# Two-layer decode attention: where the last batch's second-layer values are loaded, and when batches 0 to 6 are finished

## The chip, the core and the metric

The kernel runs on one core of a Trainium2 chip. The metric is the device time of one execution in microseconds (us). Six runs of the kernel before took 1181.73 to 1190.4 us, with a median of 1183.62 us. One execution was also profiled; all instruction times below are from it and count from its first instruction.

The core has engines that run side by side, each through its own instructions in order: PE (matmuls; PEld is its weight loads), DVE (vector), ACT (scalar), POOL (GpSimd) and SP, which here only issues DMAs. They wait for one another by semaphores.

## What is computed

Eight sequences ("batches") of one new token each pass through two layers. Both layers have the same weights and read the same key and value caches:

```
x = A_x                                    # 8 x 1 x 512
for layer in (1, 2):
    x = x + attention(layernorm(x))        # wq, K cache, V cache, wo
    x = x + silu(layernorm(x) @ w1) @ w2   # w1: 512 x 1792, w2: 1792 x 512

attention: q = (x @ wq) in 32 heads of 128; 8 groups of K and V, 4 heads each
           p = softmax(q . K * 128**-0.5)  over 8192 cached positions
           o = p . V ; result = o @ wo     # wo: 4096 x 512
```

Everything is bfloat16. For one batch and one group, K and V are 8192 x 128, that is 2 MB each. Layer 2 of a batch needs the batch's own layer 1, so values are read twice from HBM. Keys are read once, because a batch's eight groups stay on the chip between the layers.

## The kernel before

**Storage.** `kts` holds eight key slots of 2 MB, one per group. `ring` holds seven cells of 0.5 MB, of which the plan hands out six; values, four wq pieces per batch (the half of wq for groups 4 to 7) and layer-1 wo pieces go through it, in loads of one cell or of two neighbouring cells. The other half of wq, w1 and w2 stay on the chip. There are seven buffers for probabilities, `ps`: three used in turn (`N_P`) and four for deferred units (`N_DEF`).

**One unit of work** is (layer, batch, group), in two steps. `keys` (L698) expands the query (L721), spreads it into block form (L729, DVE), computes scores from the key slot (L746, 32 matmuls in four parts), takes the maximum (L758 to L767, with an all-reduce on POOL), the exponential (L772, ACT), and brings the probabilities into their buffer (L778 on PE, L785 on DVE). `values` (L819) loads V in four quarters and multiplies (L842, 8 matmuls per quarter), then reduces to one vector per head (L852, L856, L864) and normalises (L874 in layer 2). In layer 1 `turns` (L687) first transposes a key slot in place (L694).

**Passes.** The loop variable `b` runs from -1 to 7. A pass mixes layer 2 of batch `b` with layer 1 of batch `b`+1. In the middle passes the values of four second-layer groups, 4 to 7, are put off ("held") to the start of the next pass. There they load while the batch's chain runs: output of layer 1 (L960, L963), FFN (`ffn_nodes`, L481), the next norm (`norm_nodes`, L410), and the queries `queries_0` (groups 0 to 3, L642) and `queries_1` (groups 4 to 7, L665, with the four wq pieces). The pass of `b` = 7 has no layer 1 of another batch. Its order of loads is: the 16 single cells held from batch 6, single cells for groups 0 and 1 of batch 7, four wq pieces, pairs of cells for the other groups, with all of wo (two loads of 2 MB into key slots 0 and 2, `load_wo_all`, L968) put in before the sixth group.

**The end.** All eight batches' second-layer heads lie in `qab`. Eight out projections (`out_proj_b`, L924, matmuls at L933), one per group and for eight batches at once, add up in one PSUM tile. Then come the residual add (L1049), one norm and FFN for eight batches, a turn (L1058), a copy (L1066) and the store (L1080).

**The order** is not written out by hand. Each step is a node with an engine, a planned duration, a priority and dependencies. `Plan.run` (L172) plays the nodes through: each engine takes the ready node of the lowest priority number, loads go strictly in the order in which they were added, a ring load also needs free cells and gets their numbers, and a load is planned to have landed `LAND` after its transfer. The planned duration of a PE node is multiplied by `PE_SLOW`. The order that comes out is emitted once, and is then fixed for each engine. On the chip semaphores alone decide when an instruction starts. SP waits before each load until its cells or its slot were last read.

```
n = Node(name, eng, dur * (self.PE_SLOW if eng == "PE" else 1), emit, prio, deps)          # L150
heapq.heappush(events, (wire + self.LAND, seq, "done", n))                                 # L209
order = plan.run(range(N_CELL - 1))                                                        # L1071
```

Of the kernel before, what the change touches and what calls it, by code (L numbers as in the profile page):

```python
# [14 lines left out]
N_P = 3  # L15
N_DEF = 4
# [119 lines left out]
class Plan:  # L136
# [1 line left out]


    RATE = {1: 2.57, 2: 2.51, 4: 2.48}  # L140
    LAND = 2.0
    HOP = 0.1
    PE_SLOW = 1.15

    def __init__(self):
        self.nodes = []
# [104 lines left out]
def _build(ctx, nc, A_x, A_k_cache, A_v_cache, A_wq, A_wo, B_w1, B_w2, out):  # L251
# [65 lines left out]
    syn = Sync(nc, ctx)  # L317
    ksem = [DmaCounter(syn.new_sem(f"kt{i}")) for i in range(G)]
    rsem = [DmaCounter(syn.new_sem(f"ring{i}")) for i in range(N_CELL)]
    wsem = {n: DmaCounter(syn.new_sem(f"w_{n}")) for n in ("w1", "w2", "x", "wq0")}  # L320
    osem = syn.new_sem("osem")

    table = {}
# [33 lines left out]
    def gran(i, cells=1):  # L357
        return ring[:, i * GR:(i + cells) * GR]
# [51 lines left out]
    def norm_nodes(tag, prio, b0, nb, deps):  # L410
# [49 lines left out]
        def apply():  # L460
            if nb == 1:
                op(dve, lambda: dve.tensor_scalar(
                    xn[:, b0, :], xs[:, b0, :], nm, rstd[:, 0:1], op0=ALU.add, op1=ALU.mult),
                    reads=[res("xs"), res("misc"), res("rstd")], writes=[res("xn")])
            else:
                nmb = nm.unsqueeze(2).to_broadcast([128, nb, KT])
                rs = rstd[:, 0:nb].unsqueeze(2).to_broadcast([128, nb, KT])
                op(dve, lambda: dve.tensor_tensor(big_x, xs[:, bs, :], nmb, ALU.add),
                   reads=[res("xs"), res("misc")], writes=[res("ring", 1)])
                op(dve, lambda: dve.tensor_tensor(xn[:, bs, :], big_x, rs, ALU.mult),  # L470
                   reads=[res("ring", 1), res("rstd")], writes=[res("xn")])

        a = plan.add(f"{tag}.stats", "PE", 0.3, stats, prio, deps)
# [7 lines left out]
    def ffn_nodes(tag, prio, b0, nb, deps):  # L481
        bs = slice(b0, b0 + nb)
        hp = MI[:, 0:FT * nb]
        yp = MI[:, 256:256 + KT * nb]
        th, hs = (th1[:, :], hs1[:, :]) if nb == 1 else (big_th, big_hs)
        own = [] if nb == 1 else [res("ring", 1)]

        def up():
            steps = []
            for ft in range(FT):  # L490
                for kt in range(KT):
                    steps.append(lambda ft=ft, kt=kt: pe.matmul(
                        hp[:, ft * nb:(ft + 1) * nb], w1_sb[:, kt, ft * 128:(ft + 1) * 128], xn[:, bs, kt],
                        start=(kt == 0), stop=(kt == KT - 1)))
            mms(steps, reads=[res("w1"), res("xn")], writes=[res("misc")])

        def tanh():
            op(act, lambda: act.activation(th, hp, ACT.Tanh, scale=0.5),
               reads=[res("misc")], writes=[res("th")] + own)

        def gate():
            op(dve, lambda: dve.scalar_tensor_tensor(
                hs, th, 1.0, hp, op0=ALU.add, op1=ALU.mult),
                reads=[res("misc"), res("th")], writes=[res("hs")])

        def down():
            steps = []
            for dt in range(KT):
                for ft in range(FT):
                    steps.append(lambda dt=dt, ft=ft: pe.matmul(  # L510
                        yp[:, dt * nb:(dt + 1) * nb], w2_sb[:, ft, dt * 128:(dt + 1) * 128],
                        hs[:, ft * nb:(ft + 1) * nb], start=(ft == 0), stop=(ft == FT - 1)))
            mms(steps, reads=[res("w2"), res("hs")], writes=[res("misc")])

        def resid():
            yv = yp.rearrange("p (k b) -> p b k", b=nb)
            op(dve, lambda: dve.scalar_tensor_tensor(
                xs[:, bs, :], yv, 0.5, xs[:, bs, :], op0=ALU.mult, op1=ALU.add),
                reads=[res("misc"), res("xs")], writes=[res("xs")])

        n = norm_nodes(tag + ".ln", prio, b0, nb, deps)
        u = plan.add(f"{tag}.up", "PE", 1.65, up, prio, [n] + ffn_deps)
        t = plan.add(f"{tag}.tanh", "ACT", 0.2, tanh, prio, [u])
        g = plan.add(f"{tag}.gate", "DVE", 0.18, gate, prio, [t])
        d = plan.add(f"{tag}.down", "PE", 1.65, down, prio, [g])
        return plan.add(f"{tag}.resid", "DVE", 0.18, resid, prio, [d])
# [168 lines left out]
            tn.append(plan.add(f"t{b}.{g}.{q}", "DVE", T_TURN, turn, count[0] + 0.5, [kn] + tn[-1:]))  # L695
        kept[b, g] = tn

    def keys(layer, b, g, q_dep, late=None, first=False):  # L698

        u = count[0]  # L700
        count[0] += 1
        pr = FIRST + 4 if first else u
        tn = kept[b, g]
        if late is None:
            sm = plain[0] % N_P
            plain[0] += 1
        else:
            sm = N_P + late
# [29 lines left out]
        for q in range(4):  # L738
            def score(q=q):
# [3 lines left out]
                for y in range(2):  # L743
                    for t in range(4):
# [2 lines left out]
                            sc[32 * t:32 * t + 32, 0:256], w, kv[:, 2 * t + y, q],  # L747
                            start=(q == 0 and y == 0), stop=(q == 3 and y == 1)))
                mms(steps, reads=[res("kt", g), res("bd", u % N_BD)], writes=[res(*scr)], add=(q > 0))
            sn.append(plan.add(f"s{u}.{q}", "PE", 0.3, score, pr - 1,  # L750
                               [tn[3], bn] + sn[-1:]))

        if layer == 1:
# [62 lines left out]
    ot_users = []  # L816
    es = []

    def values(h, wo=None, cells=2):  # L819

        layer, b, g, u, sm = h["layer"], h["b"], h["g"], h["u"], h["sm"]
        pr = count[0] - 1
        pt, o = ps[sm], len(ot_users) % N_OT
        ot = OT[o]
        hd = slice(R * g, R * g + R)
# [2 lines left out]
        for P in range(4):  # L828
            if P == (2 if cells == 2 else 3) and wo is not None:
                h["wo"] = load_wo(wo)  # L830
            if P % cells == 0:
                vn = load_v(b, g, P, cells)

            def pv(P=P, vn=vn):


                vt = gran(vn.give, cells).rearrange("p (a c t n) -> p a c t n", a=cells, c=2, t=4)[:, P % cells]
                steps = []
                for c in range(2):
                    for t in range(4):  # L840
# [1 line left out]
                        steps.append(lambda t=t, c=c, k=k: pe.matmul(  # L842
                            ot[32 * t:32 * t + 2 * R, 0:2 * DH], pt[:, k:k + 2 * R], vt[:, c, t],
                            start=(P == 0 and c == 0), stop=(P == 3 and c == 1)))
                mms(steps, reads=cells_of(vn) + [res("p", sm)], writes=[res("ot", o)], add=(P > 0))
            n = plan.add(f"v{u}.{P}", "PE", 0.35, pv, pr, [h["exp"], vn, old or clear_n] + vs[-1:])
            if P % cells == cells - 1:
                frees(n, vn)
            vs.append(n)

# [70 lines left out]
        frees(n, wn)  # L921
        return n

    def out_proj_b(h, wn, prev):  # L924

        g = h["g"]

        def mul():
            w = slot(2 * (g // 4)).rearrange("p (h d) -> p h d", h=16)
            steps = []  # L930
            for r in range(R):
                for dt in range(KT):
                    steps.append(lambda r=r, dt=dt: pe.matmul(  # L933
                        YT[:, dt * NB:(dt + 1) * NB], w[:, R * (g % 4) + r, dt * 128:(dt + 1) * 128],
                        qab[:, :, R * g + r],
                        start=(g == 0 and r == 0 and dt == 0), stop=(g == G - 1 and r == R - 1),
                        skip_group_check=True))
            mms(steps, reads=[res("wo_all", g // 4)] + [res("attnb", g, b) for b in range(NB)],
                writes=[res("yt")], add=g > 0)
        return plan.add(f"e.w{g}", "PE", 0.56, mul, count[0] - 3, [h["n"], wn, prev])  # L940


    free_yt = [None]
# [14 lines left out]
    def x2_node(b, prio):  # L958
# [5 lines left out]
               reads=[res("ysum"), res("xs")], writes=[res("xs")])  # L964
        return plan.add(f"c{b}.x2", "DVE", 0.3, add, prio, [y_now[0]])

    wo_all = []
    def load_wo_all():  # L968
        for i in range(2):
            n = plan.load(f"woall{i}", 4, None, scored[2 * i], ring=False)  # L970

            def emit(i=i):
                dma(sp, slot(2 * i).rearrange("p (h d) -> p h d", h=16), wo_v[:, 16 * i:16 * i + 16, :], ksem[2 * i],
                    writes=[res("kt", 2 * i), res("wo_all", i)])

            n.emit = emit
            wo_all.append(n)
# [19 lines left out]
    for b in range(-1, NB):  # L997
        ready = None
        prio = FIRST
        if b >= 0:  # L1000
# [5 lines left out]
            for h in held:  # L1006
                values(h, cells=1)
                ends.append(h)
        ks, vs, held_units = pass_of(b)
        made = {}  # L1010
        todo = list(ks)

        def advance(unit):
            while unit not in made:
                k = todo.pop(0)
                layer, kb, g = k
                if layer == 0:
# [2 lines left out]
                        load_wq0()  # L1020
                        first_q.update(queries_0("f", FIRST, 0, NB, [f5]))
                    if kb == 0 and g == 4:
                        first_q.update(queries_1("f", count[0] - 5, 0, NB, [f5]))
                    made[k] = keys(0, kb, g, first_q[g])
                else:
                    if g == 4:
                        second_q.update(queries_1(f"c{b}", count[0] - 3, b, 1, [ready]))
                    made[k] = keys(1, kb, g, second_q[g], held_units.index(k) if k in held_units else None, g == 0)

        for i, v in enumerate(vs):  # L1030
            advance(vs[min(i + (1 if i == 0 and b >= 0 else 2), len(vs) - 1)])
            if b == NB - 1 and i == 5:
                load_wo_all()
            if v[0] == 0:
                a_values(made[v], cells=1 if b >= 0 and i >= len(vs) - 3 else 2)
            else:
# [4 lines left out]
            load_ffn()  # L1041


    w = free_yt[0]
    for h in ends[-G:]:
        w = out_proj_b(h, wo_all[h["g"] // 4], w)

    def e_x2():
        op(dve, lambda: dve.tensor_tensor(  # L1049
            xs[:, :, :], YT[:, 0:KT * NB].rearrange("p (k b) -> p b k", b=NB), xs[:, :, :], ALU.add),  # L1050
            reads=[res("yt"), res("xs")], writes=[res("xs")])

    big = count[0] + 10
    n = plan.add("e.x2", "DVE", 0.2, e_x2, big, [w])
    n = ffn_nodes("e", big, 0, NB, [n])

    def e_turn():
        steps = [lambda kt=kt: pe.matmul(  # L1058
# [51 lines left out]
```

## Time and profile before

| What | Value |
|---|---|
| Median of six runs | 1183.62 us |
| The profiled execution | 1184.53 us |
| Its span, first to last instruction | 1182.8 us |
| PE busy | 706.7 us (60%) |
| DVE busy | 597.7 us (51%) |
| ACT busy, POOL busy | 136.9 us, 116.8 us |
| HBM read | 465.05 MB |
| Issue to landing, median: V one cell, V two cells, a key slot | 8.2, 11.1, 11.3 us |

A row of the profile's groups reads "line engine op out<-in, shape, count, busy time, mean of one, idle time before it and who ended that". The chain of waits follows the work that ended last back to the start. In the timeline a line has the start, the duration, the engine, the line of the code and, in brackets, how long the engine had been idle and whose event ended that. "x17" after an SP line means 17 issues merged, with the waits between them in the duration.

### The profile page before, as it was taken

What the parts mean: (1) busy time and instruction counts of PE and PEld (TensorE: products, weight loads), DVE (VectorE), ACT (ScalarE), POOL (GpSimd) and SP (SyncE); (2) the same over time, 40 slices, a digit from 0 to 9 for tenths busy, and PEclk for the clock granted to TensorE, in tenths of its full rate; (3) what the DMA queues carried; (4) which work ended last, traced back from release to release, by engine and by line L of the source; (5) the groups of instructions that cost most, each with busy time, mean ns of one, the idle gap of its engine ahead of it and who ended that gap; (6) DMA issues with size and microseconds to landing.
All of it is one profiled execution on the core that took longest, in us unless ns stands there. A gap on an engine that the chain in (4) does not pass through costs nothing.

```text
span 1182.8 us, 31675 instructions
## 1 busy us (share of the span) xinstructions
PE 706.7 (60%) x13588; PEld 369.7 (31%) x13588; DVE 597.7 (51%) x1713; ACT 136.9 (12%) x475; POOL 116.8 (10%) x295
## 2 busy tenths in 40 slices
PE   2544555675565755666565766568556575666754
PEld 1222332242332423323232333224233242332433
DVE  5652467625564355733657245752556436563321
ACT  0010011111111110111111111111111111111110
POOL 1000011100110000100111000110001001010110
PEclk9666677656685666856667567775768666675775
DMA  9999799999999999999999999999999999999994
GB/s 365 421 420 353 314 421 424 411 398 409 419 416 384 382 356 415 424 406 395 420 421 411 397 408 421 421 404 405 413 402 417 390 405 422 411 405 410 347 356 177
DMA packets 86413, 467.13 MB, mean 395 GB/s; under 512 B 8944, under 2 KB 14848, under 8 KB 61952
## 3 DMA queue, kind: packets, MB, share of 16 engines
q1 hardware_dynamic: 86272, 465.10, 97.7%
q8 instruction: 107, 1.75, 0.6%
q14 instruction: 34, 0.28, 0.1%
HBM read 465.05 MB, written 0.01 MB: 393 GB/s over the span
## 4 chain that ended last, share of the span: by engine, by line
DMA 76%; PE 17%; issue 4%; DVE 2%; SPq 1%; ACT 0%; POOLq 0%; POOL 0%; ACTq 0%; DVEq 0%
DMA ring<-in_A_v_cache_dram 70%; PE ot L842 7%; PE sc L746 6%; DMA kts<-in_A_k_cache_dram 2%; DMA ring<-in_A_wq_dram 2%; DMA w<-in_B_w_dram 1%; PE misc L642 1%; DVE kts L694 1%; SPq L340 1%; PE ex L864 0%; DVE small L758 0%; PE sc L721 0%; PE yt L915 0%; PE misc L510 0%; DVE small L759 0%
## 5 line engine op out<-in xcount | busy, mean ns | idle before, releaser
L842 PE MATMUL ot<-ring,p 128*8 128x256 bf16 x4096 | 255.3, 362 | 219.3 <-DMA ring<-in_A_v_cache_dram 216.8
L694 DVE STREAM_TRANSPOSE kts<-kts 128x1024 uint32<-128x1024 uint32 x256 | 306.1, 1222 | 39.1 <-DMA kts<-in_A_k_cache_dram 38.8
L746 PE MATMUL sc<-kts,bd 128*32 128x256 bf16 x4096 | 289.4, 407 | 32.8 <-DVE kts L694 19.9
L842 PEld LDWEIGHTS ot<-ring,p 128*8 128x8 bf16 x4096 | 80.3, 92 | 312.0 <-DMA ring<-in_A_v_cache_dram 286.2
L746 PEld LDWEIGHTS sc<-kts,bd 128*32 128x32 bf16 x4096 | 115.0, 117 | 106.5 <-DVE kts L694 30.9
L856 DVE TENSOR_TENSOR part<-ot,p 128x256 bf16<-128x256 f32 x128 | 54.2, 423 | 172.4 <-ACT p L852 97.4
L763 POOL PARTITION_ALL_REDUCE small<-small x128 | 47.6, 372 | 639.8 <-DVE small L759 389.5
L772 ACT ACTIVATE expd<-sc,small 128x256 bf16<-128x256 f32 x128 | 60.6, 474 | 423.1 <-DVE small L767 384.5
L852 ACT ACTIVATE p<-ot 128x256 bf16<-128x256 f32 x128 | 49.0, 383 | 486.0 <-PE ot L842 485.2
L778 PE MATMUL sc<-expd,ident 128*32 128x256 bf16 x512 | 41.9, 316 | 94.4 <-ACT expd L772 89.2
L758 DVE TENSOR_REDUCE small<-sc 128x1 f32<-128x256 f32 x128 | 53.2, 416 | 52.9 <-PE sc L746 52.7
L792 POOL PARTITION_ALL_REDUCE small<-small x128 | 55.1, 431 | 214.5 <-DVE small L788 214.5
L729 DVE TENSOR_TENSOR bd<-sc,mask 128x64 bf16<-128x64 f32 x128 | 27.7, 217 | 83.3 <-PE sc L746 74.2
L785 DVE STREAM_TRANSPOSE p<-sc 128x256 bf16<-128x256 bf16 x128 | 56.9, 444 | 8.2 <-PE sc L778 5.7
L778 PEld LDWEIGHTS sc<-expd,ident 128*32 128x32 bf16 x512 | 15.3, 109 | 126.1 <-ACT expd L772 124.2
L788 DVE TENSOR_SCALAR small<-hm,small 128x4 f32<-128x4 f32 x128 | 26.5, 207 | 33.6 <-ACT expd L772 33.5
L864 PE MATMUL ex<-diag,p 128*128 128x4 bf16 x256 | 26.3, 172 | 24.4 <-DVE part L856 23.1
L915 PEld LDWEIGHTS yt<-z,ring 128*128 128x128 bf16 x1024 | 31.3, 100 | 26.6 <-issue 26.1
L864 PEld LDWEIGHTS ex<-diag,p 128*128 128x128 bf16 x256 | 16.5, 105 | 73.5 <-issue 39.1
L915 PE MATMUL yt<-z,ring 128*128 128x4 bf16 x1024 | 36.2, 166 | 5.5 <-DVE z L893 4.0
L767 DVE SCALAR_TENSOR_TENSOR small<-small,hm 128x4 f32<-128x4 f32 x128 | 19.4, 151 | 37.9 <-POOL small L763 37.7
L759 DVE TENSOR_SCALAR small<-hneg,small 128x4 f32<-128x4 f32 x128 | 29.4, 230 | 4.5
(82 smaller groups left out, 434.7 us busy)
## 6 DMA issues: line engine op xcount, KB each, us to landing
ring<-in_A_v_cache_dram SPq DMA_DIRECT2D x260, 512.0 KB, 8.2
kts<-in_A_k_cache_dram SPq DMA_DIRECT2D x64, 2048.0 KB, 11.3
ring<-in_A_v_cache_dram SPq DMA_DIRECT2D x126, 1024.0 KB, 11.1
ring<-in_A_wo_dram SPq DMA_DIRECT2D x64, 512.0 KB, 11.3
ring<-in_A_wq_dram SPq DMA_DIRECT2D x36, 512.0 KB, 9.3
kts<-in_A_wo_dram SPq DMA_DIRECT2D x2, 2048.0 KB, 16.0
w<-in_B_w_dram SPq DMA_DIRECT2D x2, 1792.0 KB, 12.8
wq<-in_A_wq_dram SPq DMA_DIRECT2D x4, 512.0 KB, 11.2
```

The lines of the kernel that those rows point to most:

```text
L694: op(dve, lambda: dve.transpose(v, v), reads=[], writes=[res("kt", g)], add=(q > 0))
L746: steps.append(lambda t=t, y=y, w=w: pe.matmul(sc[32 * t:32 * t + 32, 0:256], w, kv[:, 2 * t + y, q], start=(q == 0 and y == 0), stop=(q = ...
L758: op(dve, lambda: dve.tensor_reduce(mxr[si], sv, AX.X, ALU.max), reads=[res(*scr)], writes=[res("mxr", si)])
L763: op(pool, lambda: pool.partition_all_reduce(mxa[si], mxp[si], 128, bass.bass_isa.ReduceOp.max), reads=[res("mxp", si)], writes=[res("mxa" ...
L772: op(act, lambda: act.activation(pe_out[:, :], sv, ACT.Exp, bias=bias[si], scale=SM_SCALE, accum_out=rsum[si]), reads=[res(*scr), res("bia ...
L778: steps = [lambda P=P: pe.matmul(sc[32 * P:32 * P + 32, 256:512], src[:, P], pe_out[:, :], start=True, stop=True) for P in range(4)]
L785: op(dve, lambda: dve.transpose(pt[:, :], src), reads=[res(*scr)], writes=[res("p", sm)])
L792: op(pool, lambda: pool.partition_all_reduce(ssa[si], ssm[si], 128, bass.bass_isa.ReduceOp.add), reads=[res("mxp", si)], writes=[res("mxa" ...
L842: steps.append(lambda t=t, c=c, k=k: pe.matmul(ot[32 * t:32 * t + 2 * R, 0:2 * DH], pt[:, k:k + 2 * R], vt[:, c, t], start=(P == 0 and c = ...
L852: op(act, lambda: act.activation(pt[:, :], ot[:, 0:2 * DH], ACT.Copy), reads=[res("ot", o)], writes=[res("p", sm)])
L856: op(dve, lambda: dve.tensor_tensor(part[:, :], ot[:, 0:2 * DH], pt[:, :], ALU.subtract), reads=[res("ot", o), res("p", sm)], writes=[res( ...
L915: steps.append(lambda j=j, dt=dt: pe.matmul(YT[:, dt * R:(dt + 1) * R], w[:, j, dt * 128:(dt + 1) * 128], zt[:, R * j:R * j + R], start=(g ...
```

## The change

The pass of `b` = 7 is written anew, and the plan's constants are changed.

- The wq pieces for groups 4 to 7 come directly after the held cells of batch 6, ahead of every value of batch 7.
- The keys of groups 0 to 6 get the seven probability buffers 0 to 6, and group 7 gets buffer 0 after group 0's values.
- Values of groups 0 and 1 still go through the ring, in single cells. Values of groups 2, 3, 4 go into key slots 0, 1, 2 and those of groups 5, 6, 7 into slots 5, 6, 7, each as one 2 MB load; the last as loads of 1 MB, 0.5 MB and 0.5 MB with semaphores of their own. A slot is loaded after the scores that read it.
- wo goes into slots 3 and 4 and loads between the values of groups 4 and 5.
- The out projection runs twice: for batches 0 to 6 ("d", 28 columns) with its own residual add, norm and FFN at low priority, and for batch 7 ("e", 4 columns) at the end. So the FFN and norm take 7 batches and 1, where they took 8.
- Plan: `LAND` 5.0 for 2.0, `PE_SLOW` 1.0 for 1.15, a score part 0.45 for 0.3, a value quarter 0.4 for 0.35. `queries_1` also depends on the copy of `queries_0`.

```diff
-    LAND = 2.0
+    LAND = 5.0
     HOP = 0.1
-    PE_SLOW = 1.15
+    PE_SLOW = 1.0
...
-    def keys(layer, b, g, q_dep, late=None, first=False):
+    def keys(layer, b, g, q_dep, late=None, first=False, buf=None):
...
-        if late is None:
+        if buf is not None:
+            sm = buf
+        elif late is None:
...
-            sn.append(plan.add(f"s{u}.{q}", "PE", 0.3, score, pr - 1,
+            sn.append(plan.add(f"s{u}.{q}", "PE", 0.45, score, pr - 1,
...
+    def load_v_slot(b, g, k):
+        parts = (2, 1, 1) if g == G - 1 else (4,)
+        src = A_v_cache[b, g].rearrange("(p y) d -> p (y d)", p=128)
+        got = []
+        for i, cells in enumerate(parts):
+            q = sum(parts[:i])
+            where = res("vs", k, i)
+            def emit(i=i, q=q, cells=cells, where=where):
+                dma(sp, slot(k)[:, GR * q:GR * (q + cells)], src[:, GR * q:GR * (q + cells)],
+                    ksem[k] if len(parts) == 1 else wsem[f"end{i}"],
+                    writes=[where] + ([res("kt", k)] if i == 0 else []))
+            n = plan.load(f"v{b}.{g}.{q}", cells, emit, scored[k], ring=False)
+            got += [(n, slot(k)[:, GR * (q + j):GR * (q + j + 1)], where) for j in range(cells)]
+        return got
...
-        pr = count[0] - 1
+        pr = count[0] - 1 if b < NB - 1 else u + 1
+        quarters = load_v_slot(b, g, at) if at is not None else None
...
-            n = plan.add(f"v{u}.{P}", "PE", 0.35, pv, pr, [h["exp"], vn, old or clear_n] + vs[-1:])
+            n = plan.add(f"v{u}.{P}", "PE", 0.4, pv, pr, [h["exp"], vn, old or clear_n] + vs[-1:])
...
-        return plan.add(f"e.w{g}", "PE", 0.56, mul, count[0] - 3, [h["n"], wn, prev])
+        return plan.add(f"{tag}.w{g}", "PE", 0.56, mul, count[0] + (20 if nb > 1 else 0), deps)
...
+    WO_AT = (3, 4)
...
+        if b == NB - 1:
+            break
...
+    fin = NB - 1
+    second_q.update(queries_1(f"c{fin}", FIRST + 6, fin, 1, [ready, second_q[3]]))
+    made = [keys(1, fin, g, second_q[g], first=g == 0, buf=g % (N_P + N_DEF)) for g in range(G - 1)]
+    values(made[0], cells=1)
+    made.append(keys(1, fin, G - 1, second_q[G - 1], buf=0))
+    values(made[1], cells=1)
+    for g, k in ((2, 0), (3, 1), (4, 2)):
+        values(made[g], at=k)
+    load_wo_all()
+    for g, k in ((5, 5), (6, 6), (7, 7)):
+        values(made[g], at=k)
     w = free_yt[0]
-    for h in ends[-G:]:
-        w = out_proj_b(h, wo_all[h["g"] // 4], w)
...
+    done = [h["n"] for h in ends] + [made[1]["n"]]
+    for g in range(G):
+        w = out_proj_b("d", g, 0, fin, [w, wo_all[g // 4]] + done)
+    n = x2_of("d", 0, fin, count[0] + 20, [w])
+    fed = ffn_nodes("d", count[0] + 20, 0, fin, [n, second_q[G - 1]])
+    w = n
+    for g in range(G):
+        w = out_proj_b("e", g, fin, 1, [made[g]["n"], w])
     big = count[0] + 10
-    n = plan.add("e.x2", "DVE", 0.2, e_x2, big, [w])
-    n = ffn_nodes("e", big, 0, NB, [n])
+    n = x2_of("e", fin, 1, big, [w])
+    n = ffn_nodes("e", big, fin, 1, [n, fed])
```

## The prediction

> **What bounds the kernel now.** I read the page first. Its DMA row and its chain of waits name the resource.
>
> ```profile
> DMA  9999799999999999999999999999999999999994
> ...
> DMA 76%; PE 17%; issue 4%; DVE 2%; SPq 1%; ACT 0%; POOLq 0%; POOL 0%; ACTq 0%; DVEq 0%
> ```
>
> The 16 DMA engines are nine tenths busy or more in all slices but two, the fifth and the last; 465.05 MB are read in a span of 1182.8 us, 393 GB/s on average. The change moves no byte less, so time can come only from stretches in which the queue runs below its rate, and from the compute after the last landing. Next I cut the span at the moments when each batch's second-layer query is computed (123.3, 260.2, 401.5, ...), so that each row is one pass of the steady loop. Columns: stretch, its length, busy time and count of PE, PEld, DVE, ACT, POOL, granted clock, DMA share, GB/s.
>
> ```profile
> core 0: us, PE busy (x) PEld busy (x) DVE busy (x) ACT busy (x) POOL busy (x), PEclk, DMA share, GB/s
> 401.50:543.40 141.90, 86.58 (x1651) 44.46 (x1649) 74.04 (x211) 17.05 (x60) 13.98 (x34) 0.67 0.99 399
> 543.40:682.10 138.70, 87.51 (x1650) 44.62 (x1648) 73.86 (x211) 16.95 (x60) 13.97 (x34) 0.64 1.01 409
> 682.10:819.90 137.80, 86.86 (x1648) 44.20 (x1646) 73.96 (x211) 16.75 (x60) 13.98 (x34) 0.70 1.02 413
> ```
>
> Six alike passes take 141.3, 141.9, 138.7, 137.8, 140.3 and 139.9 us (mean 140.0): the same work, up to 4.1 us apart. That spread is what the order on PE and the state of the ring cost or save. Then the end, in stretches:
>
> ```profile
> 1100.00:1130.00 30.00, 22.93 (x496) 13.55 (x493) 10.41 (x49) 4.49 (x15) 3.84 (x10) 0.82 0.89 318
> 1130.00:1140.00 10.00, 7.13 (x144) 3.35 (x136) 5.65 (x27) 2.17 (x8) 2.15 (x7) 1.00 1.01 412
> 1140.00:1153.00 13.00, 3.08 (x97) 2.63 (x98) 1.00 (x4) 0.38 (x1) 0.42 (x1) 0.57 1.09 366
> 1153.00:1166.00 13.00, 6.43 (x122) 2.94 (x118) 1.17 (x4) 0.77 (x2) 0.00 (x0) 0.50 0.99 398
> 1060.00:1100.00 40.00, 26.06 (x518) 12.56 (x515) 13.09 (x42) 4.38 (x17) 2.75 (x6) 0.54 1.02 400
> ```
>
> Between 1100 and 1130 us the queue moves only 318 GB/s. The order of SP's issues says why:
>
> ```profile
> 1074.42 36.83 SPq L340 DMA_DIRECT2D ring<-in_A_v_cache_dram  x25
> 1111.73 2.91 SPq L340 DMA_DIRECT2D ring<-in_A_wq_dram  x4
> 1117.12 16.23 SPq L340 DMA_DIRECT2D ring<-in_A_v_cache_dram  x6
> 1133.41 7.13 SPq L340 DMA_DIRECT2D kts<-in_A_wo_dram  x2
> 1140.64 21.53 SPq L340 DMA_DIRECT2D ring<-in_A_v_cache_dram  x6
> ```
>
> The last eight of the 25 single cells are the last batch's groups 0 and 1. They fill the six-cell ring before its probabilities exist (first use at 1110.44), and the four wq pieces, which groups 4 to 7 wait for, stand behind them until 1111.73. SP's waits in 1100 to 1130 are 21.1 us on "PE ot L842" and 3.0 on "PE misc L665": all are ring cells not yet freed. Last, the tail after the last landing, out of the timeline:
>
> ```profile
> 1167.48 1.02 PE L842 MATMUL ot<-ring,p 128*8 128x256 bf16 x16 [0.80 <-DMA ring<-in_A_v_cache_dram]
> ...
> 1170.75 0.19 DVE L1049 TENSOR_TENSOR xs<-yt,xs 128x32 bf16<-128x32 f32 x1 [0.69 <-PE yt L933]
> ...
> 1173.39 1.69 POOL L457 TENSOR_TENSOR rstd<-var,expo 128x8 f32<-128x8 f32 x1 [32.97 <-DVE ring L468]
> ...
> 1181.09 0.31 SPq L1080 DMA_DIRECT2D out_dram<-ring  x1
> ```
>
> From the last landing to the store are 13.6 us of pure chain, 8.76 of them from the residual add (1170.75) to the end of the eight-batch FFN (1179.51).
>
> **What the Trainium skill says.** "DMA: Bandwidth & Descriptors", section "Anatomy of one DMA", says that DMA engines do not wait on semaphores: the wait happens on the issuing sequencer. The trace agrees: the hole at 1100 to 1130 is SP standing before a ring cell.[...] "TensorE: Matmul & The Clock Gate", section "Part 2: What happens when you issue a matmul", says that matmuls stay in program order and only weight loads are pulled ahead. The trace agrees: at 419.81 PE resumes after 6.41 us of waiting for a value cell. This is why a changed plan, which fixes that order, can matter at all.
>
> **The change part by part.** *Query weights first (the wq loads now stand before all values of the last batch).* The wq pieces take the ring places that groups 0 and 1 blocked. A wq cell is freed by its own matmul (0.55 to 0.60 us) as soon as it lands, with no wait for a softmax. No instruction is added.
>
> *Values into key slots.* Groups 2 to 7 (6 x 2.10 = 12.58 MB) no longer need ring cells; SP waits for the slot's scores instead. In the trace slot 0 is scored by about 1104 and eight groups of scores end at 1137.8 although groups 4 to 7 start only at 1124; with wq earlier they start about 10 us sooner, so each slot is free well before its load's turn (the first at about 1117, then one per 5 us). The queue can then hold megabytes instead of 3.1. Behind SP's wait on a slot are only later loads of the same queue.
>
> *The sum for the queue.* Left from 1100 to 1166: 318 x 30 + 412 x 10 + 366 x 13 + 398 x 13 = 23.6 MB, of which wo is 4.2. After: 12.6 MB of values in slots at 412 GB/s (the 1130 row; the best pass has 413) are 30.5 us; wo at 350 (the slices in which only wo is moved show 345 to 360) 12.0; the other 6.8 MB in single cells at 400 (the 1060 row) 17.0. Sum 59.6 against 66: at most 6.4 us. SP issues nothing between about 1099.9 and 1103.9 because PE is in the second query (1.42) and the first scores when cells would come free; that stays. I keep 1.4 us of loss for it and take 5.0. Bounds: 0 (the hole only moves) to 6.4.
>
> *Seven probability buffers and the late eighth group.* Group 7 takes buffer 0 after group 0's values. Its wait is for about 1118, its values land last: hidden by some 40 us of loads. Cost 0.
>
> *Batches 0 to 6 finished while values load.* Added: eight more 16-matmul out projections (0.60 each, 4.8 us), one more add, norm and FFN. All need wo, whose second half lands about 6.3 MB before the end (15.3 us, so about 1145 when the queue ends at 1160). After that half: four projections 2.4, add 0.2, norm and FFN of seven 8.5 (from the 8.76 above), so it ends at about 1156.5, some 4 us before the last cell. The value matmuls it meets on PE (2.4 us per group per 5 us) have room. Cost 0; without that cover it would be up to 8 us.
>
> *The tail, for one batch.* The last load is one cell, so its matmuls take 0.60 (the 8-fold rows) for 1.02: -0.4. Squares: six matmuls for 48, variance starts 0.57 after the statistics for 1.74: -1.2. Variance is one 0.29 instruction for three (0.66 to the start of POOL against 0.38): -0.3. POOL's power 0.58 (the one-batch rows) for 1.69: -1.1. Normalise 0.28 for 0.19: +0.1. Tanh, gate and residual 0.18, 0.17, 0.16 for 0.26, 0.27, 0.19: -0.2. Sum -3.1. The last group's projection (0.60), the turn and the store stay.
>
> *The plan (landings 5 for 2, PE factor 1.0 for 1.15, scores 0.45, values 0.4).* It issues nothing, adds nothing and does not change the order of loads, but it redraws PE's and DVE's order and which ring cell a load gets, in all passes. The trace of before shows no other plan. By its six passes: every pass like the best is 6 x 2.2 = -13 us, every pass like the worst is 0.6 + 0 + 3.2 + 4.1 + 1.6 + 2.0 = +11.5. I see no reason for a sign: the PE factor moves the plan towards the measured durations (up matmuls 1.63, planned 1.90 before and 1.65 after), the landing moves value matmuls later in PE's order, where a cell waits longer to be freed. I take 0.
>
> Sum: -5.0 - 3.1 = -8.1. The profiled execution took 1184.53 (span 1182.8), so 1176.4; it lay 0.9 above the median 1183.62, from which it is 1175.5. Forecast 1176.
>
> **Rivals.** *The plan slows every pass.* Value matmuls planned later stand behind scores or query matmuls on PE, ring cells come back late, and SP starves the queue while the held groups load, as at 430 to 440 us now, where 170 and 310 GB/s are moved. For it: passes 2 and 3 show such a loss of 4 us. Against it: most of the time a 2.10 MB key load queues behind, and hides it. At 1.2 us per pass over seven passes it eats the gain; from 1.7 it is slower than before; at the worst pass everywhere it gives 1176.4 + 11.5 = 1188.
>
> *The plan helps every pass.* The same spread the other way: the hole at 430 to 440 goes, 1176.4 - 13 = 1163. For it: planned durations are nearer the measured ones. Against it: 413 GB/s would have to be held in all passes.
>
> *The hole only moves.* Group 0's probabilities come late after the query (in this trace POOL starts the first maximum 2.65 us after its input, 0.6 in the pass before), the six cells fill with wq and group 0, and slots begin late. Then only the tail counts: 1184.5 - 3.1 = 1181.4. It is also the time if the batch 0 to 6 work ends some 5 us after the last cell.
>
> **How the numbers follow.** Chances: forecast 0.50 (own range 1172 to 1180), plan slows 0.20, plan helps 0.15, hole moves 0.15. A measurement of this kernel can tell a change from none at about 0.3%, 3.6 us. Eight in ten: I cut the far half of the helping case and the far part of the slowing one: 1166 to 1188. Faster by over 0.3%: 0.48 + 0.15 + 0.06 + 0.02 = 0.71; within: 0.02 + 0.07 + 0.03 = 0.12; slower: 0.02 from the forecast's edge and 0.15 from the slow plan = 0.17.
>
> **What would show it.** Queue: GB/s of the 30 us after the last second-layer query over 390 instead of 318, wq issued before the last eight single cells, values into kts without a wait of SP over 3 us. Tail: from the last landing to the store 10.5 us instead of 13.6, POOL's last power near 0.6. Covered work: the seven-batch FFN ends before the last value cell lands. Plan: the mean of the six passes stays within 1 us of 140.0; if it moves by more, my zero was the wrong step, and its sign decides whether the forecast falls high or low.

## The result and the profile after

The changed kernel's median is 1178.85 us (21 runs, 1172.12 to 1184.85), that of the kernel before, measured beside it, 1184.21 us (42 runs). The ratio is 0.9947, 95% interval [0.9932, 0.9962]: 5.4 us less by the medians, 4.5 to 8.1 us by the interval. The profiled execution took 1176.79 us with a span of 1174.7.

The page's DMA row and chain look as before; 465.05 MB are read in a shorter span:

```profile
DMA  9999799999999999999999999999999999999994
...
DMA 80%; PE 15%; issue 2%; DVE 1%; SPq 1%; ACT 0%; POOL 0%; POOLq 0%; DVEq 0%
```

SP's issues of the last batch, from the timeline:

```profile
1093.20 6.85 SPq L340 DMA_DIRECT2D ring<-in_A_wq_dram  x4
1100.66 9.51 SPq L340 DMA_DIRECT2D ring<-in_A_v_cache_dram  x8
1110.22 1.65 SPq L340 DMA_DIRECT2D kts<-in_A_v_cache_dram  x3
1113.18 19.56 SPq L340 DMA_DIRECT2D kts<-in_A_wo_dram  x2
1132.83 7.71 SPq L340 DMA_DIRECT2D kts<-in_A_v_cache_dram  x5
```

The wq pieces go first, and by 1113 three whole groups are queued. The stretches after the last second-layer query (1095.75 in this profile) show a fuller queue (columns: stretch, length, busy time of five engines, granted clock, DMA share, GB/s):

```profile
1096.00:1126.00 30.00, 26.87 (x555) 13.89 (x552) 13.41 (x65) 5.37 (x18) 5.20 (x13) 0.94 1.01 400
1126.00:1158.00 32.00, 17.74 (x461) 12.54 (x458) 5.46 (x25) 2.32 (x9) 2.77 (x4) 0.57 1.00 378
```

The first row answers to the 318 GB/s of 1100 to 1130 before; a small hole is left in it, 324 GB/s from 1100 to 1105. The end, from the timeline:

```profile
1144.66 1.87 PE L961 MATMUL yt<-qab,kts 128*128 128x7 bf16 x64 [4.05 <-DMA kts<-in_A_wo_dram]
...
1149.86 1.54 POOL L457 TENSOR_TENSOR rstd<-var,expo 128x7 f32<-128x7 f32 x1 [19.67 <-DVE ring L468]
...
1154.20 1.60 PE L492 MATMUL misc<-xn,w 128*128 128x7 bf16 x54
...
1156.97 0.21 PE L492 MATMUL misc<-xn,w 128*128 128x7 bf16 x2 [1.17 <-issue]
...
1158.85 1.65 PE L510 MATMUL misc<-ring,w 128*128 128x7 bf16 x56
1160.43 2.73 PE L871 MATMUL ot<-kts,p 128*8 128x256 bf16 x48
...
1166.51 0.55 POOL L457 TENSOR_TENSOR rstd<-var,expo 128x1 f32<-128x1 f32 x1 [15.12 <-DVE var L447]
...
1172.97 0.31 SPq L1128 DMA_DIRECT2D out_dram<-ring  x1
```

The second half of wo is used at 1144.66, but the seven-batch FFN is at its down projection (L510; L492 is the up projection) only at 1158.85. Behind it stand 48 value matmuls (L871), those of the last group among them. No idle time stands before them: the last packet had come at 1159.48.

**How I compare sections.** Single profiled executions differ by several us in the part before the last batch, so I cut each at two moments: the 48 matmuls of the last second-layer query (L642), and the end of the last value packet, from the packet records of the trace.

| us | query at | query to last packet | packet to last value matmul's end | from there to the store | query to store |
|---|---|---|---|---|---|
| before | 1099.96 | 67.1 | 1.4 | 12.6 | 81.1 |
| changed | 1095.61 | 63.9 | 3.7 | 9.8 | 77.4 |

(The 48 matmuls are taken from PE's timeline, where the group starts up to 0.15 us before its row in the chain.) The queue gained 3.3 us, the chain after the last value matmul 2.8, and the wait for that matmul lost 2.3.

### The profile page after: what moved, and what is told of

Same layout as the page of the kernel before. It is cut to its first block, busy times and chain, and to the rows that moved or that the text cites. A ratio compares the mean times of both kernels' runs of the same rounds, so it can differ in the third digit from the quotient of the medians.

```text
span 1174.7 us, 32188 instructions
## 1 busy us (share of the span) xinstructions
PE 716.7 (61%) x13836; PEld 373.4 (32%) x13836; DVE 599.4 (51%) x1718; ACT 138.2 (12%) x477; POOL 117.0 (10%) x296
## 3 DMA queue, kind: packets, MB, share of 16 engines
HBM read 465.05 MB, written 0.01 MB: 396 GB/s over the span
## 4 chain that ended last, share of the span: by engine, by line
DMA 80%; PE 15%; issue 2%; DVE 1%; SPq 1%; ACT 0%; POOL 0%; POOLq 0%; DVEq 0%
DMA ring<-in_A_v_cache_dram 74%; PE ot L871 8%; PE sc L748 4%; DMA kts<-in_A_wo_dram 2%; DMA ring<-in_A_wq_dram 2%; DMA w<-in_B_w_dram 1%; PE misc L642 1%; PE yt L944 1%; DMA kts<-in_A_v_cache_dram 1%; PE sc L723 1%; SPq L340 0%; PE ex L893 0%; PE ex L915 0%; PE misc L510 0%; DVE part L885 0%
## 5 line engine op out<-in xcount | busy, mean ns | idle before, releaser
L871 PE MATMUL ot<-ring,p 128*8 128x256 bf16 x3904 | 242.6, 359 | 195.8 <-DMA ring<-in_A_v_cache_dram 194.7
L694 DVE STREAM_TRANSPOSE kts<-kts 128x1024 uint32<-128x1024 uint32 x256 | 309.2, 1227 | 39.3 <-DMA kts<-in_A_k_cache_dram 38.7
L871 PEld LDWEIGHTS ot<-ring,p 128*8 128x8 bf16 x3904 | 73.0, 90 | 280.8 <-DMA ring<-in_A_v_cache_dram 261.4
L922 DVE TENSOR_TENSOR z<-ex,rc 128x16 bf16<-128x16 f32 x64 | 11.1, 174 | 54.5 <-PE ex L915 54.4
L723 PE MATMUL sc<-qab,sel 128*128 128x4 bf16 x256 | 16.3, 170 | 31.4 <-DVE rc L798 21.1
```

What stands on the lines that cost most here:

```text
L694: op(dve, lambda: dve.transpose(v, v), reads=[], writes=[res("kt", g)], add=(q > 0))
L871: steps.append(lambda t=t, c=c, k=k: pe.matmul(ot[32 * t:32 * t + 2 * R, 0:2 * DH], pt[:, k:k + 2 * R], vt[:, c, t], start=(P == 0 and c = ...
```

## The experiments

All rows are of the same cuts; the ratio is to the kernel before, measured beside it. Before itself had medians of 1186.59 us beside e1 to e4, 1187.41 beside e5 to e8 and 1184.91 beside e9 to e12, so single "query at" figures of different rows do not compare to a us or two.

| run | query at | query to packet | packet to matmul | query to store | ratio and interval |
|---|---|---|---|---|---|
| e1 plan only | 1100.15 | 66.9 | 1.4 | 80.8 | 0.9974 [0.9951, 0.9997] |
| e2 old plan | 1098.99 | 62.7 | 1.7 | 74.7 | 0.9942 [0.9918, 0.9967] |
| e3 no split | 1099.89 | 62.9 | 1.1 | 76.6 | 0.9949 [0.9931, 0.9967] |
| e4 wo early | 1105.18 | 63.7 | 2.2 | 75.7 | 0.9915 [0.9883, 0.9946] |
| e5 seven batches first | 1098.20 | 63.4 | 5.0 | 78.2 | 0.9951 [0.9932, 0.9969] |
| e6 wq late | 1091.72 | 63.5 | 3.5 | 76.8 | 0.9947 [0.9927, 0.9967] |
| e7 old plan, wo early | 1098.20 | 63.0 | 1.1 | 73.9 | 0.9940 [0.9914, 0.9967] |
| e8 changed, again | 1101.37 | 63.5 | 4.6 | 77.9 | 0.9949 [0.9933, 0.9964] |
| e9 last loads held back | 1102.54 | 63.9 | 4.4 | 78.1 | 0.9954 [0.9938, 0.9970] |
| e10 landing 2 | 1100.16 | 63.7 | 3.6 | 77.1 | 0.9969 [0.9950, 0.9987] |
| e11 old plan, wo earlier | 1099.86 | 63.0 | 0.9 | 73.6 | 0.9945 [0.9927, 0.9964] |
| e12 values in the ring | 1105.18 | 65.4 | 1.4 | 79.4 | 0.9973 [0.9956, 0.9990] |

**e1 and e2: the plan alone, and the last batch alone.** e1 is the kernel before with the new constants; e2 is the changed kernel with

```diff
-    LAND = 5.0
+    LAND = 2.0
     HOP = 0.1
-    PE_SLOW = 1.0
+    PE_SLOW = 1.15
```

and the old durations of scores and values.

> The kernel before with the plan's constants of the change alone (landing 5, PE factor 1, scores 0.45, values 0.4, second half of the query after the first). Theory A, the plan redraws the order but is worth nothing on the mean: ratio to before 1.000, between 0.998 and 1.002, and the tail from the last traffic to the store stays 14.7 us. Rival B, the 4 us by which the passes up to 1100 us were shorter in the changed kernel's profile come from the plan: ratio 0.9965.

> The changed kernel with the old plan constants (landing 2, PE factor 1.15, scores 0.3, values 0.35). Theory A: the last batch's own changes carry the gain, ratio to before 0.995 like the whole change, and 30 us after the last second-layer query still at 400 GB/s. Rival B, the plan carries it: ratio 0.998 to 1.000.

e2 is clear: without the new plan the gain is all there, and the last section is even 2.7 us shorter. e1 lies between its two numbers, and its interval reaches both: its last section is as before (80.8), yet its ratio's upper end is below 1.000. What it gained would lie before the last query. Its profile has the query at 1100.15 against 1099.96, but before was 2.4 us slower beside e1 than beside the changed kernel (1186.59 against 1184.21), so these two moments cannot settle it.

**e8: the changed kernel once more.**

> The changed kernel once more, unaltered, to see how far one profile can be trusted. Theory A, the part up to the last second-layer query scatters by several us from execution to execution whatever the plan (1095.8 in its first profile, 1100 to 1105 in others with the same order up to there), while the last section repeats: query at 1097 to 1104, section 76.5 to 78.5 us, ratio 0.995. Rival B, the plan makes the first part shorter: query at 1095 to 1097 again.

The query came at 1101.37 where the first profile had 1095.61, while the last section repeats to 0.5 us. So 4 us between two profiles at the query show nothing of a plan. The last section can be compared from single profiles, to about half a us as far as this one pair tells; its parts move more (3.7 and 4.6 us from packet to matmul).

**e3: all eight batches finished together.**

```diff
-    for g in range(G):
-        w = out_proj_b("d", g, 0, fin, [w, wo_all[g // 4]] + done)
...
+    for g in range(G):
+        w = out_proj_b("e", g, 0, NB, [made[g]["n"], wo_all[g // 4], w])
+    n = x2_of("e", 0, NB, big, [w])
+    n = ffn_nodes("e", big, 0, NB, [n])
```

> The changed kernel, but all eight batches are finished together at the end, as before. Theory A, the split costs more than it saves since the seven-batch FFN comes late on PE and holds up the last value matmuls: from the last traffic to the store 14.3 us (the 14.7 of before less 0.4 for the smaller last load) where the changed kernel has 15.9, so 1.6 us faster than the changed kernel, ratio to before 0.993. Rival, the split pays the 3.1 us that I forecast and something else delays the end: 17 us or more from the last traffic to the store, ratio 0.997.

The last section is 0.8 to 1.3 us shorter without the split, and the ratio is the changed kernel's. From the last packet to the store it took 13.7 us; the changed kernel's two profiles have 13.5 and 14.4 (the 15.9 in the expectation counted from an earlier moment of the fading traffic). So the tail is about even, and most of the difference lies ahead of the last packet (62.9 us after the query, for 63.9 and 63.5). e2, e7 and e11 have 62.7 to 63.0 there, too; why is open. The value matmuls now follow their landing:

```profile
1160.85 1.03 PE L871 MATMUL ot<-kts,p 128*8 128x256 bf16 x16 [0.62 <-DMA kts<-in_A_v_cache_dram]
...
1163.30 0.60 PE L871 MATMUL ot<-kts,p 128*8 128x256 bf16 x8
```

So what the split's short chain saves at the end (9.8 us for 12.6) is paid back in front of it (3.7 and 4.6 us for 1.1).

**e4, e5, e7, e11: when the seven-batch work runs.** e4 loads wo ahead of group 4's values; e7 does it with the old constants; e11 ahead of group 3's, with the old constants:

```diff
-    for g, k in ((2, 0), (3, 1), (4, 2)):
+    for g, k in ((2, 0), (3, 1)):
         values(made[g], at=k)
     load_wo_all()
-    for g, k in ((5, 5), (6, 6), (7, 7)):
+    for g, k in ((4, 2), (5, 5), (6, 6), (7, 7)):
```

> The changed kernel with wo loaded ahead of group 4's values instead of behind them, so that it lands some 5 us earlier and the seven-batch norm and FFN can be done before the last two groups land. Theory A, late seven-batch work on PE is what lengthens the tail: from the last traffic to the store 11.5 to 13 us instead of 15.9, ratio to before 0.992. Rival, the last value matmuls are late for another reason (their own planned place): the tail stays at 15 to 16 us and the ratio at 0.995.

> The changed kernel with the old plan constants and wo ahead of group 4's values. With the old constants alone the section from the last second-layer query to the store took 74.7 us, and the seven-batch down projection (1.65) still stood between the last value matmul and the last out projection. Theory A: with wo earlier it is done before, so 73 us and a ratio to before of 0.992. Rival: the section is set by the last traffic alone and stays at 74.5 us or more.

> The changed kernel with the old constants and wo loaded after group 2's values, one group earlier still (73.9 us for the section with wo after group 3, 74.7 after group 4). Theory A, PE at half clock is full while the last three groups land and earlier wo spreads that work: the tail from the last value packet to the store, 10.9 us with wo after group 3, is 10.5 to 11, section 73.5 to 74. Rival, the slots 3 and 4 are not scored in time and SP waits: section 75 us or more. Ratio to before 0.992 to 0.994.

Earlier wo takes most of the wait away: 2.2, 1.1 and 0.9 us from the last packet to the last value matmul's end, and 12.0, 10.9 and 10.7 us from the last packet to the store. All three sections fall on the side of Theory A. In the timed runs only e4 points that way: the ratios of e7 and e11 are that of e2, 0.994. In e7 PE itself waits for the last value cell again, and the down projection is long done:

```profile
1154.55 0.34 PE L510 MATMUL misc<-ring,w 128*128 128x7 bf16 x7 [1.38 <-issue]
...
1161.01 0.39 PE L871 MATMUL ot<-kts,p 128*8 128x256 bf16 x8
1161.67 0.59 PE L871 MATMUL ot<-kts,p 128*8 128x256 bf16 x8 [0.27 <-DMA kts<-in_A_v_cache_dram]
...
1163.85 0.59 PE L961 MATMUL yt<-qab,kts 128*128 128x1 bf16 x16 [0.26 <-DVE qab L903]
```

e5 instead gives the seven-batch nodes the first place among what is ready (`count[0] - 100` for `count[0] + 20`).

> The changed kernel, with the seven-batch projections, norm and FFN planned ahead of all other work that is ready (priority far below the values' instead of far above). The section from the last second-layer query (48 matmuls at L642) to the store took 77.4 us in the changed kernel. Theory A, the late seven-batch work is what holds up the last values: the last value matmul ends under 2 us after the last value packet (3.7 in the changed kernel) and the section is 75 to 76 us. Rival, early seven-batch work only delays the values in another place: the section stays at 77 us or grows.

Theory A fails and the rival holds: 5.0 us of wait, 78.2 us. First place does not help, because PE has little room. In the changed kernel's 15 us before the end of the traffic PE is busy, at a granted clock of 0.50:

```profile
1145.00:1150.00 5.00, 4.31 (x146) 3.80 (x142) 0.77 (x5) 0.23 (x1) 0.14 (x1) 0.50 1.00 419
1150.00:1155.00 5.00, 4.40 (x106) 2.71 (x105) 0.38 (x2) 0.38 (x1) 1.39 (x1) 0.50 0.98 406
1155.00:1160.00 5.00, 3.83 (x112) 2.87 (x109) 0.62 (x3) 0.25 (x1) 0.00 (x0) 0.50 0.44 177
```

That is 12.5 of 15 us, and two idle times of 0.60 and 1.17 us are marked "issue", so 14.3 are taken. Spreading the work over more time, by an earlier wo, makes room. So does another order of the same work: e2, with wo where the change has it, puts the 48 value matmuls ahead of the down projection, and its last packet is 12.0 us before the store, as in e4:

```profile
1159.61 2.73 PE L871 MATMUL ot<-kts,p 128*8 128x256 bf16 x48
...
1163.45 1.63 PE L510 MATMUL misc<-ring,w 128*128 128x7 bf16 x56
```

**e10: which constant.** The changed kernel with the planned landing at 2.0 alone.

> The changed kernel with the planned landing at 2.0 again and the other new constants kept. With all the old constants the section from the last second-layer query to the store took 74.7 us instead of 77.4 to 77.9. Theory A, the landing of 5 puts the last values behind the seven-batch work: 74.5 to 75.5 us. Rival, the PE durations do it: 77 us or more.

The rival holds: 77.1 us, and the order up, two value quarters, down, 48 value matmuls is as in the changed kernel. The landing is not what puts the seven-batch work late. The planned PE durations are: e2 differs from e10 in them alone and has another order and 74.7 us. I did not separate the factor from the score and value times.

**e6 and e12: what fills the queue.** e6 puts the four wq pieces behind the values of groups 0 and 1. e12 is e3 with all values in pairs of ring cells (`values(made[g])` without `at`).

> The changed kernel, but with the four wq pieces behind the values of groups 0 and 1, as before the change. Theory A, the order of wq against these eight cells made the hole: the 30 us after the last second-layer query fall from 399 GB/s to between 320 and 350 and the section from that query to the store grows from 77.4 to 80 to 82 us. Rival C, the key slots as a second place for values made the gain whatever the order: 385 GB/s or more and at most 78.5 us.

> The changed kernel without two of its parts: all values of the last batch go through the ring in pairs of cells, and the eight batches are finished together. Kept are wq first, the seven probability buffers, wo in slots 3 and 4 and the new plan. With the slots (and no split) the last value packet came 62.9 us after the last second-layer query. Theory A, the slots are what fills the queue: 66 to 67 us, as before the change (67.1). Rival, wq first and the seven buffers fill it: 64 us or less.

e6 refutes Theory A: wq was issued after the eight single cells (the window cuts the first row short), and the 30 us after the query still move 397 GB/s:

```profile
1090.91 10.07 SPq L340 DMA_DIRECT2D ring<-in_A_v_cache_dram  x7
1101.36 3.32 SPq L340 DMA_DIRECT2D ring<-in_A_wq_dram  x4
1104.73 1.37 SPq L340 DMA_DIRECT2D kts<-in_A_v_cache_dram  x3
```

Directly behind wq stand three 2 MB loads that need no ring cell. e12, without the slots, starts at 384 GB/s but then falls to 350, where the changed kernel has 370 from 1125.61 to 1159:

```profile
1105.32:1135.30 29.98, 27.95 (x597) 15.52 (x593) 14.86 (x70) 5.65 (x19) 5.63 (x14) 0.91 1.00 384
1135.30:1171.00 35.70, 12.90 (x264) 6.89 (x268) 3.68 (x15) 2.10 (x6) 0.80 (x2) 0.53 0.96 350
```

e12's 65.4 us fall between its two theories. Of the 4.2 us that e3's queue gains over before, the slots carry 2.5 (65.4 to 62.9); the remaining 1.7 belong to what e12 keeps (wq first, seven buffers, wo's slots, the plan) together.

**e9: holding the last loads back.** In the changed kernel the traffic fades over some 4 us; before it fell from 385 to 115 to 0 GB/s in three steps of 1 us:

```profile
1154.00:1155.00 1.00, 1.00 (x38) 0.80 (x31) 0.19 (x1) 0.38 (x1) 0.00 (x0) 0.50 1.05 418
1155.00:1156.00 1.00, 0.81 (x31) 0.72 (x27) 0.23 (x1) 0.00 (x0) 0.00 (x0) 0.50 0.90 356
1156.00:1157.00 1.00, 0.03 (x1) 0.03 (x2) 0.00 (x0) 0.00 (x0) 0.00 (x0) 0.50 0.64 262
1157.00:1158.00 1.00, 1.00 (x21) 0.56 (x22) 0.39 (x2) 0.25 (x1) 0.00 (x0) 0.50 0.40 164
```

e9 lets SP issue group 7's loads only when group 5 has landed (`reads=[res("vs", 5, 0)]` on those loads).

> The changed kernel, with the three loads of group 7 issued only when group 5's values have landed. In the changed kernel the traffic ebbs over the last 4 us (418, 356, 262, 164, 90, 12 GB/s by the us), where before it stopped within 1.5 us. Theory A, the engines drift apart behind a deep queue: with a shallower queue the ebb is 2 us or less and the last value packet comes 61.5 to 62.5 us after the last second-layer query instead of 63.5 to 63.9. Rival, an engine that is slow stays slow whatever is queued: 63.3 us or more.

SP now took 18.64 us for the last five issues instead of 7.71, and the last packet still came at 63.9. By that the rival holds. The fade itself got shorter, some 2.5 us:

```profile
1163.00:1164.00 1.00, 0.16 (x6) 0.07 (x3) 0.00 (x0) 0.00 (x0) 0.00 (x0) 0.50 0.99 393
1164.00:1165.00 1.00, 0.41 (x10) 0.39 (x14) 0.00 (x0) 0.15 (x1) 0.00 (x0) 0.50 0.40 164
1165.00:1166.00 1.00, 1.00 (x28) 0.56 (x24) 0.39 (x2) 0.10 (x1) 0.00 (x0) 0.50 0.28 115
```

So a shallower queue ends no earlier. Nor do the slots make the fade: e1, which loads like the kernel before, falls from 344 GB/s (1163.5 to 1164) to 115 in the next half us and fades to 16 (1166.5 to 1167). What makes it stays open.

## Why the prediction was right, and where its steps were not

The forecast of 1176 against 1178.85, with the sign and the size about right, is in part luck. The sum for the last batch was -8.1 us, and its section measured -3.8 and -3.3 (81.1 against 77.4 and 77.9): the queue's gain was put too high and the seven-batch work was put at nothing. That the whole still came within 3 us is because the plan, a third term put at zero, likely gave some 2.5 us.

*The queue, -5.0: measured -3.3 and -3.7.* The rate was right (399 GB/s in the 30 us after the query, forecast over 390). What the sum left out is the end: a mean rate up to the last byte, while from 1155 on the traffic fades. 0.88 MB move from 1155 to 1160, which 412 GB/s would take 2.1 us for, and the last packet ends 4.5 us after 1155. That covers the miss in size; no run took the fade away to prove it. The prediction's first reason was also wrong: e6 shows that with the slots in place wq first is worth nothing measurable, and the slots are the larger part.

*The seven-batch work, "cost 0": measured 2.6 and 3.6 us* (3.7 and 4.6 from packet to matmul, against 1.1 in e3, which has the same last load and no split). This is the step that failed. wo landed when I said (1144.66, forecast about 1145), the norm and FFN were forecast done at 1156.5, and the last add ran at 1160.54. The prediction added up the chain's own durations and judged PE's room by the value matmuls alone. It named eight added out projections but left batch 7's, 0.58 each and six of them in this stretch, out of that room, and it knew neither of the two issue stalls nor that the plan would put all four quarters of group 5 ahead of the up projection. e2, e3, e4, e7 and e11 show it from three sides: with another order, without the split, or with wo earlier, the time from packet to matmul shrinks to between 0.9 and 2.2 us.

*The tail's chain, -3.1:* holds. From the last value matmul's end to the store 12.6 became 9.8 and, in the second profile, 9.75; the forecast for that part is -2.7, the other -0.4 being the smaller last load (1.4 us from packet to matmul before, 1.1 in e3). But the 10.5 us forecast from the last landing to the store were 13.5 and 14.4 from the last packet (14.0 before), because of the wait in front. POOL's last power took 0.55 (0.58 forecast).

*The plan, 0 with both signs open:* the profiles alone agree with 0. The six passes took 139.0 us on the mean of the changed kernel's first profile, within the 1 us of 140.0 that the prediction allowed. The last second-layer query came at 1100.0 us on the mean of nine profiles with landing 5 (1091.7 to 1105.2) and at 1099.4 of five with landing 2, before among them. But those nine executions ran 0.7 us above their kernels' medians on the mean, and those five 1.6 us below; less this, the query came at 1099.3 and 1101.0.

The timed runs say the same more sharply. Take each ratio's gain (times 1185 us) less the gain of its last section: the nine measurements with landing 5 leave 1.4 to 4.7 us unexplained, 2.5 on the mean; the four with landing 2 (e2, e7, e10, e11) leave -1.0 to 0.5. Each alone is no better than its interval, some 2 to 4 us to either side, but the two groups do not overlap, and within each set of runs measured beside one another (e1 to e4, e5 to e8, e9 to e12) they lie the same way. So the landing of 5 is likely worth some 2.5 us ahead of the last query, and the changed kernel's 6 us are about 3.5 from the last batch and 2.5 from the plan. That is argued from this grouping, not shown by one run. The grouping was made after the results, and no trace shows where in the passes the time is saved: one profile of a kernel scatters by more than that.

*The slower rival,* a plan that costs 1.2 us or more per pass, did not happen. *The hole that only moves* did not either, though the late seven-batch work, which that rival named, did.

The best version measured is e4: 0.9915 [0.9883, 0.9946], six runs. Its interval touches the changed kernel's, so that it is better is likely but not settled; its last section is 1.7 to 2.2 us shorter. e7 and e11 have the shortest last sections, with the plan that seems worse ahead of it. Landing 5 with the old PE durations and an early wo was not tried.

## What to carry to other kernels

When the data have landed but the last matmuls have not run, look at what stands before them on the same engine, and add up that engine's whole work in that stretch at the clock it is granted there, not the added chain alone. Work meant to hide behind loads must have its own last input early enough; moving that input's load forward helped (e4, e7), and so did putting the last value matmuls ahead of it (e2); putting it ahead of everything did not (e5). And where one execution scatters by more than the effect, cut the traces at events and compare sections.

## What the runs showed of the hardware that was not expected

- **PE stalls marked "issue" follow instruction packets.** In the changed kernel 16 KB packets of the instruction queue ended at 1149.22 and 1155.60, and PE resumed from its two stalls at 1150.76 and 1156.97, that is 1.54 and 1.37 us later. In all ten kernels with the split (the changed kernel, e2, e4 to e11) each "issue" stall over 0.3 us from 1090 on, 19 in all, ends 1.25 to 1.54 us after such a packet. The four profiles without the split (before, e1, e3, e12) have no such stall there. The largest is in e4, in the middle of a down projection:

```profile
1162.40 0.54 PE L510 MATMUL misc<-ring,w 128*128 128x7 bf16 x14 [1.85 <-issue]
```

 That PE waits there for its own instructions is inferred from these times; no run varied it.

- **An issue can hold its queue for long.** SP's issue of the second wo half, whose packets are 1 KB, took 15.7 us in the changed kernel and the next one 5.79, where most take 0.33 to 0.45. The view of waits names a DVE event, but the ends fit landings: the issue of the second wo half ended at 1132.74, when the last value load ahead of wo landed (1132.75), the next issue at 1138.62, when the first wo half landed (1138.69). In all 14 profiles the two ends lie within 0.2 and 0.4 us of these two landings. It looks as if SP could finish issuing the second wo half only once the first was alone in the queue, and the next load only once the first had landed; that is inferred from times. The transfers did not suffer: 411 to 433 GB/s from 1115 to 1130.

- **The traffic fades at its end.** In the changed kernel the mean busy share of the 16 engines falls over 0.90, 0.64, 0.40, 0.25 and 0.03 in the last 5 us, so not all of them work to the end; which ones stop is not recorded here; the fade took about 1.5 us in the profile of before, 3 in e1 and 2.5 in e9.
